# The first keys in two transfers, and two output tiles in one store

## The chip, the cores and the metric

The kernel runs on one core of one Trainium2 chip. The metric is the device time of one launch in microseconds (us). Several runs are made and their median counts.

## The reference, cut to what matters

Inputs: `q`, `k`, `v` of shape (8, 8, 576, 64) (batch, heads, sequence, head size), `phi` (512, 32), `w1` (8, 512, 1024), `w2` (8, 1024, 512), all float32. The output is (4608, 512) float32.

```
k_p, v_p = mean of k, v over groups of 8 neighbouring rows          # 576 -> 72 rows
attn     = softmax(q @ k_p^T / 8) @ v_p                             # pooled attention
x        = attn, heads side by side                                 # (4608, 512)
logits   = x @ phi                                                  # (4608, 32), 4 slots for each of 8 experts
d        = softmax of logits over the 4608 tokens
slots    = d^T @ x                                                  # 32 slot inputs
slot_out = relu(slots @ w1[e]) @ w2[e]   for the 4 slots of each expert e
out      = softmax of logits over the 32 slots  @  slot_out         # (4608, 512)
```

## The kernel before, in words

**Loads.** All of `q`, `k`, `v` and the weights are read once. Nearly all loads are issued by GpSimd (POOL), whose queue turns float32 into bfloat16 on the way; they stand in one queue (q0 in the profile) in the order of issue, and each is issued as soon as its buffer is free. `big` has four buffers for two batches (a "pair") of `q`, `k` or `v` each, 128 rows of 72 x 64 values; later the weights `w1` (`w_sb` in the profile) and `w2` follow, `w2` into buffers that the attention has left (`big`, `qTa`, `xsa`).

**The first keys.** One part of the first load goes another way. Of each of the 128 rows of pair 0 of `k`, the first `CUT` = 2048 values (8 KB of float32) are loaded by SyncE (SP; queue q1 in the profile) as float32 into `kf`, a piece of the tile `exa` that is not in use yet (L117 to L119). VectorE (DVE) and ScalarE (ACT) turn one half each into bfloat16 (L149, L150). The other 2560 values of each row come through POOL's queue (L120), and behind that load, in this order, stand the first `q`, `phi`, the first `v` and the second `k`. The engines meanwhile fill constants. TensorE (PE) begins when `phi` has been spread by DVE (L179): its first products are those of L184, between which the pooling of the first keys (L232) begins.

**Attention.** For each pair the keys and values are pooled and turned by PE, then scores (L309), exponentials (ACT, L311) and the product with the values (L331) run in a pipeline, written out in the order in which the engines are to work. PE's last use of a buffer releases POOL's next load.

**The end.** The last weights, of `w2`, come in two halves of 256 columns: first all pieces of the left half, then all of the right (L533). Into `so_ps` the second layer is summed. `begin(0, ...)` (L655) starts the output for the left half: it scales `so_ps` (`so_a`), makes the products of the first four tiles of 128 rows, scales them by `put` on ACT or DVE, and stores them with `store` (L635), which SP issues. `put(0)`, `put(1)` and `put(2)` of the left half are on ACT, one behind the other, `put(3)` is on DVE. Then `tiles` makes further left tiles, the right half's pieces are summed, `begin(1, ...)` starts the right half, and the remaining 26 tiles follow with all 512 columns and three large stores, of 8, 16 and 28 KB for each of 128 rows. A left or right tile is a store of 1 KB for each of 128 rows. All stores stand in q1.

**Order.** POOL's instructions, and from L546 those of all engines, stand in the order in which they are written; before that a planner orders the other engines, each of which then works in that order. A DMA counts up a semaphore when it has landed; SP's 16 DMAs use eight such semaphores in turn, so the ninth waits until the first has landed, and so on.

Of the kernel before, what the change touches and what calls it, by code (L numbers as in the profile page):

```python
# [18 lines left out]
def kernel(  # L19
# [10 lines left out]
    nc = tc.nc  # L30

    B, H, S, D = q.shape
# [51 lines left out]
    def pair_of(src, pair):  # L84
        return src[2 * pair:2 * pair + 2].rearrange("b h (i t) d -> (b h i) (t d)", t=NT)
# [30 lines left out]

    CUT = 4 * POOL * D  # L117
    kf = exf[:, 0:CUT]
    nc.sync.dma_start(out=kf, in_=pair_of(k, 0)[:, 0:CUT])  # L119
    nc.gpsimd.dma_start(out=big[:, 0, CUT:KQ], in_=pair_of(k, 0)[:, CUT:KQ])  # L120
    q_sb, k_sb, v_sb = {}, {}, {}
    k_sb[0] = big[:, 0].rearrange("p (t d) -> p t d", d=D)
# [41 lines left out]
    with tc.tile_pool(name="tmp", bufs=1) as tmp:  # L164
# [8 lines left out]
        for r in range(2):  # L173
            rows = slice(r * D, (r + 1) * D)
            nc.vector.tensor_copy(out=iphi[rows, :, r, 0:D],
                                  in_=ident[rows, rows].rearrange("p d -> p () d").to_broadcast([D, HQ, D]))
# [279 lines left out]
    def of_tile(t, n):  # L456
        g, r = TILES[n]
        rows, base = GROUPS[g]
        step, c0 = rows // 2, base // 2 + r // 2
        return t[:, r % 2, c0:c0 + 127 * step + 1:step]  # L460

    def tokens(n):

        return of_tile(cT, n)
# [64 lines left out]
    for half, cols in enumerate(halves):  # L529
        for e, j0, j1 in PIECES:  # L530
# [3 lines left out]
                                in_=moe_w2[e].rearrange("(p j) d -> p j d", j=FJ)[:, j0:j1, cols])  # L534
# [44 lines left out]
    def second_layer(e, j0=0, j1=FJ, half=None, by=1):  # L579

        cols = slice(0, DM) if half is None else halves[half]
        for fj in range(j0, j1):
            g = fj % NG
            rhs = w2_at[e, fj] if half is None else w2_half[e, fj, half]
            nc.tensor.matmul(out=so_ps[g * NS:(g + 1) * NS, cols].rearrange("p (c s) -> p s c", s=by), lhsT=hT[:, e, fj],  # L585
                             rhs=rhs.rearrange("p (c s) -> p s c", s=by),
                             start=(e == 0 and fj < NG), stop=(e == E - 1 and fj >= NG), skip_group_check=True)
# [29 lines left out]
    def scaled(engine, dst, src, by):  # L617
        if engine == 0:
            nc.scalar.activation(out=dst, in_=src, func=AF.Copy, scale=by)  # L619
        else:  # L620
            nc.vector.tensor_scalar(out=dst, in0=src, scalar1=by, scalar2=None, op0=ALU.mult)  # L621
# [13 lines left out]
    def store(g, r0, r1, cols):  # L635
        home, dst = places[g]
        nc.sync.dma_start(out=dst[:, r0:r1, cols], in_=home[:, r0:r1, cols])
# [13 lines left out]
    def put(n, cols, engine, ps):  # L651
        g, r = TILES[n]
        scaled(engine, places[g][0][:, r, cols], ps, rec(n))

    def begin(half, stores):  # L655

        cols = halves[half]
        scaled(0, so_a[:, cols], so_ps[:, cols], recC)
        f = []
        for n in range(CARRY):  # L660
            f.append(ps_f.tile([128, DM], FP, name="f_ps", tag="f")[:, 0:HC])
            nc.tensor.matmul(out=f[n], lhsT=of_tile(zT, n), rhs=w2_half[E - 1, J7, half],
                             start=True, stop=False)
        for n in range(CARRY):
            nc.tensor.matmul(out=f[n], lhsT=tokens(n), rhs=so_a[:, cols], start=False, stop=True)
            if n == (0 if half == 0 else CARRY - 1):
                second_layer(E - 1, J7, FJ, half)
        put(0, cols, 0, f[0])
        if half == 0:
            scaled(1, so[:, cols], so_ps[:, cols], recC)  # L670
            put(1, cols, 0, f[1])
            put(2, cols, 0, f[2])
            put(3, cols, 1, f[3])
        else:
            put(1, cols, 1, f[1])
            put(2, cols, 0, f[2])
            scaled(1, so[:, cols], so_ps[:, cols], recC)
            put(3, cols, 0, f[3])
        for r0, r1 in stores:
            store(0, r0, r1, cols)  # L680
# [22 lines left out]
    second_layer(*PIECES[1], 0)  # L703
    busy(192)
    second_layer(*PIECES[2], 0)
    begin(0, ((0, 1), (1, 2), (2, 4)))
    for n in (4, 6):
        tiles(n, n + 2, 0)
    for e, j0, j1 in PIECES[:2]:
# [42 lines left out]
```

## Time and profile before

| | us |
|---|---|
| median of 3 runs | 174.14 |
| lowest and highest | 174.07, 174.61 |
| the profiled execution, its own time | 174.13 |
| span of its instructions | 172.3 |
| PE busy | 131.0 |
| DVE busy | 100.6 |
| ACT busy | 88.1 |
| POOL busy | 27.5 |

The profile is of one execution. All times in it count from the first instruction of the program, and the execution's own time has 1.8 us more than the span, before and behind it. "DMA share" is the time that packets took as a share of 16 DMA engines; where two packets of one engine overlap it passes 1. GB/s counts the bytes that are written: for a load that turns float32 into bfloat16, half of what is read. A packet is here one row of a transfer.

### The profile page before, as it was taken

To read this page: it belongs to the slowest core of one execution; us is meant where nothing else is said; L and a number is where in the kernel's file an instruction comes from. 1 tells how busy PE (TensorE), PEld (TensorE's weight loads), DVE (VectorE), ACT (ScalarE), POOL (GpSimd) and SP (SyncE) were. 2 spreads that over 40 slices of the span, in tenths; PEclk is the share of its full clock that TensorE was granted. 3 is DMA by queue.
4 is the path that set the end of the run, shared out by engine and by line. 5 is a ranking of instruction groups with operands and counts; after the bars stand their busy time and mean duration, and the time that the engine had idled before them with its cause. 6 is when DMAs were issued, how large, how long until landed. Compare 5 with 4: busy or idle time off the path is not lost.

```text
span 172.3 us, 2868 instructions
## 1 busy us (share of the span) xinstructions
PE 131.0 (76%) x1106; PEld 70.1 (41%) x1106; DVE 100.6 (58%) x265; ACT 88.1 (51%) x168; POOL 27.5 (16%) x42
## 2 busy tenths in 40 slices
PE   0005778899999999999789999887899998799100
PEld 0002353565555655556345554462442235343000
DVE  6686263478779658887975868750650102599300
ACT  3201337977686937988503998555021004799100
POOL 7000111022101032207001471120501030000000
PEclk9999999999999999999999999999999999999955
DMA  5999999999999999999999999999999999999994
GB/s 184 252 218 225 210 216 220 215 216 214 214 216 220 209 224 208 220 218 216 215 213 215 217 213 221 215 219 219 215 215 215 206 196 195 322 369 436 479 426 213
DMA packets 10589, 41.13 MB, mean 239 GB/s; under 512 B 704, under 2 KB 6592, under 8 KB 6864
## 3 DMA queue, kind: packets, MB, share of 16 engines
q0 software_dynamic: 7248, 30.48, 87.1%
q1 hardware_dynamic: 3328, 10.49, 15.5%
q8 instruction: 8, 0.13, 0.3%
q14 instruction: 5, 0.04, 0.1%
HBM read 61.93 MB, written 9.44 MB: 414 GB/s over the span
## 4 chain that ended last, share of the span: by engine, by line
PE 33%; DMA 28%; DVE 15%; ACT 12%; issue 3%; POOL 1%; DVEq 0%; POOLq 0%; ACTq 0%
DMA xsa<-in_moe_w_dram 21%; PE pool_ps L232 10%; DMA phi_f<-in_moe_phi_dram 7%; ACT exa L311 7%; DVE xsa L342 6%; PE u_ps L331 5%; PE sc L309 5%; PE q_ps L264 4%; DVE w_sb L621 4%; PE G_ps L366 3%; PE turn_ps L248 2%; ACT vmeans L238 2%; DVE rsum L240 2%; ACT vp L296 2%; DVE rec L336 2%
## 5 line engine op out<-in xcount | busy, mean ns | idle before, releaser
L311 ACT ACTIVATE exa<-sc 72x576 bf16<-72x576 f32 x64 | 39.3, 653 | 4.6 <-PE sc L309 3.8
L342 DVE TENSOR_TENSOR xsa<-u_ps,rec 128x384 bf16<-128x384 f32 x69 | 37.8, 554 | 1.7
L331 PE MATMUL u_ps<-vp,exa 128*128 128x97 bf16 (+5 forms) x320 | 31.3, 229 | 3.6 <-DVE xsa L342 3.0
L331 PEld LDWEIGHTS <-exa 128*128 128x128 bf16 (+1 forms) x320 | 18.9, 100 | 15.7 <-DVE xsa L342 6.5
L309 PE MATMUL sc<-qTa,kp 64*72 64x288 bf16 x128 | 20.5, 303 | 1.7 <-ACT exa L311 1.3
L232 PE MATMUL pool_ps<-big,pmat 128*128 128x512 bf16 x64 | 18.2, 411 | 0.7 <-ACT qTa L268 0.6
L336 DVE RECIPROCAL rec<-u_ps 128x4 f32<-128x4 f32 x72 | 11.9, 175 | 10.8 <-PE u_ps L331 10.5
L184 PE MATMUL phi_ps<-spread,sel 128*128 128x256 bf16 x4 | 1.3, 396 | 15.0 <-DVE spread L179 15.0
L268 ACT COPY qTa<-q_ps 128x768 bf16<-128x768 bf16 x8 | 6.3, 794 | 12.3 <-PE q_ps L264 12.3
L621 DVE TENSOR_SCALAR w_sb<-f_ps,recR 128x512 f32<-128x512 f32 (+1 forms) x19 | 11.3, 660 | 1.5 <-DMA xsa<-in_moe_w_dram 0.7
L264 PE MATMUL q_ps<-ident,big 128*128 128x128 bf16 x144 | 11.6, 219 | 0.8 <-DVE qTa L270 0.3
L309 PEld LDWEIGHTS <-kp 64*72 64x72 bf16 x128 | 7.7, 106 | 8.9 <-issue 3.5
L240 DVE TENSOR_REDUCE rsum<-rest_ps 128x64 f32<-128x512 f32 x8 | 5.5, 692 | 10.0 <-PE rest_ps L236 9.9
L642 PE MATMUL f_ps<-so,cT 128*128 128x512 bf16 (+1 forms) x38 | 10.1, 361 | 1.6 <-DVE so L621 0.9
L619 ACT ACTIVATE w_sb<-f_ps,recR 128x512 f32<-128x512 f32 (+1 forms) x19 | 10.3, 620 | 1.3 <-PE f_ps L642 1.1
L270 DVE COPY qTa<-q_ps 128x768 bf16<-128x768 bf16 x16 | 8.7, 551 | 2.3 <-PE q_ps L264 2.2
L264 PEld LDWEIGHTS <-big 128*128 128x128 bf16 x144 | 8.7, 97 | 3.0 <-issue 1.4
L533 POOL DMA_DIRECT2D xsa<-in_moe_w_dram x8 | 5.9, 744 | 23.2 <-DMA qTa<-in_moe_w_dram 8.9
L366 PE MATMUL G_ps<-xsa,ee 128*128 128x512 bf16 x36 | 8.4, 379 | 1.2 <-ACT ee L361 1.2
L232 PEld LDWEIGHTS <-pmat 128*128 128x128 bf16 x64 | 6.0, 103 | 6.8 <-issue 2.3
L619 ACT ACTIVATE so_a<-so_ps,recC 128x256 bf16<-128x256 f32 x2 | 0.9, 474 | 13.8 <-PE so_ps L585 13.8
L238 ACT CAST vmeans<-pool_ps 128x1024 bf16<-128x1024 f32 x4 | 4.0, 1012 | 6.8 <-PE pool_ps L232 6.8
(109 smaller groups left out, 166.8 us busy)
## 6 DMA issues: line engine op xcount, KB each, us to landing
w_sb<-in_moe_w_dram POOLq DMA_DIRECT2D x2, 3072.0 KB, 37.6
big<-in_q_dram POOLq DMA_DIRECT2D x4, 1152.0 KB, 12.7
big<-in_v_dram POOLq DMA_DIRECT2D x4, 1152.0 KB, 16.5
big<-in_moe_w_dram POOLq DMA_DIRECT2D x1, 4096.0 KB, 34.2
out_dram<-w_sb SPq DMA_DIRECT2D x1, 3584.0 KB, 10.2
big<-in_k_dram POOLq DMA_DIRECT2D x3, 1152.0 KB, 21.3
w_sb<-in_moe_w_dram POOLq DMA_DIRECT2D x2, 1024.0 KB, 19.2
qTa<-in_moe_w_dram POOLq DMA_DIRECT2D x1, 2048.0 KB, 30.9
```

Of the source, the lines that this page charges most:

```text
L232: nc.tensor.matmul(out=ps, lhsT=pmat, rhs=src[:, t:full * POOL:POOL, :], start=(t == 0), stop=(t == POOL - 1))
L240: nc.vector.reduce_sum(out=rsum, in_=rest.rearrange("p t d -> p d t"), axis=AX.X)
L264: nc.tensor.transpose(out=ps[:, t].rearrange("p n i -> p (n i)"), in_=q_sb[pair][:, tt:tt + 2, :].rearrange("p t d -> p (t d)"), identity= ...
L309: nc.tensor.matmul(out=ps[:, r, 0:S // 2], lhsT=kp[pair][rows, n], rhs=qT[pair][rows, n].rearrange("p t i -> p (t i)"), start=True, stop=True)
L311: nc.scalar.activation(out=dst.rearrange("p r (i t) -> p r i t", t=NU), in_=ps[:, :, 0:S // 2].rearrange("p r (t i) -> p r i t", i=NI), fu ...
L331: nc.tensor.matmul(out=bank[rows, hh * UW:(hh + times) * UW].rearrange("p (a c) -> p a c", a=times), lhsT=ex[b][:, hh].rearrange("p r t -> ...
L336: nc.vector.reciprocal(out=rec, in_=ps[:, :, XW])
L342: nc.vector.tensor_tensor(out=dst, in0=ps[:, :, 0:XW], in1=rec.rearrange("p h -> p h ()").to_broadcast([128, HQ, XW]), op=ALU.mult)
L366: nc.tensor.matmul(out=ps, lhsT=ee[:, t].rearrange("p g s -> p (g s)"), rhs=x[:, t, :, 0:D], start=(t == 0), stop=(t == 8))
L619: nc.scalar.activation(out=dst, in_=src, func=AF.Copy, scale=by)
L621: nc.vector.tensor_scalar(out=dst, in0=src, scalar1=by, scalar2=None, op0=ALU.mult)
L642: nc.tensor.matmul(out=bank[:, 0:times * (cols.stop - cols.start)].rearrange("p (a c) -> p a c", a=times), lhsT=tokens(n), rhs=rhs.rearran ...
```

## The change

The load of the first keys by SP is cut in two: first 256 values (1 KB) of each of the 128 rows, then the other 1792 (7 KB) of each. The casts of L149 and L150 wait for both. And the left half of the first two output tiles, until now two stores, is stored by one. SP has 16 DMAs as before, and the order of the instructions on the other engines is the same.

```diff
     CUT = 4 * POOL * D
     kf = exf[:, 0:CUT]
-    nc.sync.dma_start(out=kf, in_=pair_of(k, 0)[:, 0:CUT])
+
+    AHEAD = 4 * D
+    for c0, c1 in ((0, AHEAD), (AHEAD, CUT)):
+        nc.sync.dma_start(out=kf[:, c0:c1], in_=pair_of(k, 0)[:, c0:c1])
     nc.gpsimd.dma_start(out=big[:, 0, CUT:KQ], in_=pair_of(k, 0)[:, CUT:KQ])
...
     second_layer(*PIECES[2], 0)
-    begin(0, ((0, 1), (1, 2), (2, 4)))
+    begin(0, ((0, 2), (2, 4)))
     for n in (4, 6):
         tiles(n, n + 2, 0)
```

## The prediction

> **What bounds the kernel now.** I read the page first, its slices, its queues and its chain, and then the DMA share by stretches of time.
>
> ```profile
> DMA  5999999999999999999999999999999999999994
> GB/s 184 252 218 225 210 216 220 215 216 214 214 216 220 209 224 208 220 218 216 215 213 215 217 213 221 215 219 219 215 215 215 206 196 195 322 369 436 479 426 213
> q0 software_dynamic: 7248, 30.48, 87.1%
> q1 hardware_dynamic: 3328, 10.49, 15.5%
> DMA xsa<-in_moe_w_dram 21%; PE pool_ps L232 10%; DMA phi_f<-in_moe_phi_dram 7%; ACT exa L311 7%; DVE xsa L342 6%; PE u_ps L331 5%; PE sc L309 5%; PE q_ps L264 4%; DVE w_sb L621 4%; PE G_ps L366 3%; PE turn_ps L248 2%; ACT vmeans L238 2%; DVE rsum L240 2%; ACT vp L296 2%; DVE rec L336 2%
> ```
>
> The reader is to see two things. In the DMA row only the first and the last slice are below 9. And q0 with 87.1% and q1 with 15.5% fill the 16 DMA engines for the whole span. The chain names many lines, but its largest piece is a load of weights, which lands when it does because everything ahead of it in the queue has been moved. By stretches:
>
> ```profile
> 1.00:1.50 0.50, 0.00 (x0) 0.00 (x0) 0.48 (x1) 0.50 (x1) 0.27 (x1) 1.00 0.00 0
> 1.50:2.00 0.50, 0.00 (x0) 0.00 (x0) 0.47 (x2) 0.50 (x1) 0.50 (x2) 1.00 1.28 213
> 1.50:2.50 1.00, 0.00 (x0) 0.00 (x0) 0.47 (x2) 0.72 (x2) 1.00 (x3) 1.00 0.86 164
> 2.50:3.50 1.00, 0.00 (x0) 0.00 (x0) 0.94 (x1) 0.00 (x0) 0.93 (x3) 1.00 0.81 295
> 3.50:4.50 1.00, 0.00 (x0) 0.00 (x0) 1.00 (x1) 0.00 (x0) 1.00 (x3) 1.00 1.01 426
> 5.50:8.50 3.00, 0.00 (x0) 0.00 (x0) 2.18 (x3) 1.04 (x1) 0.00 (x0) 1.00 1.09 225
> 24.00:128.00 104.00, 94.31 (x906) 54.82 (x906) 70.60 (x196) 68.69 (x132) 21.39 (x27) 1.00 1.03 216
> 150.00:151.00 1.00, 0.35 (x4) 0.36 (x4) 0.66 (x2) 0.78 (x3) 0.00 (x0) 1.00 0.98 342
> 154.00:170.00 16.00, 5.33 (x18) 2.10 (x17) 7.11 (x11) 6.09 (x11) 0.00 (x0) 0.78 1.06 445
> ```
>
> The last two columns are DMA share and GB/s. From 3.5 us to 170 us the share is 1 or above, with one stretch at 0.98. So the DMA engines are the bound, and the time is: when they reach full rate, plus bytes and packets over the rate. A microsecond that they lose or win at the start is carried to the end, and a microsecond of another engine counts only where it leaves them without work. That is the rule by which I cost both edits.
>
> **The start, as it is.** The queue view of the same stretches (packets, MB, share; 1.5 to 2.5, 2.5 to 3.5, 3.5 to 4.5, then both queues of 4.5 to 5.5), and who issues and who waits in the timeline:
>
> ```profile
> q1 hardware_dynamic: 20, 0.16, 86.1%
> q1 hardware_dynamic: 36, 0.29, 80.9%
> q1 hardware_dynamic: 52, 0.43, 101.0%
> q0 software_dynamic: 27, 0.14, 68.4%
> q1 hardware_dynamic: 36, 0.16, 39.5%
> ```
>
> ```profile
> 0.74 0.37 SPq L119 DMA_DIRECT2D exa<-in_k_dram  x1
> 1.23 0.67 POOL L120 DMA_DIRECT2D big<-in_k_dram  x1 [0.79 <-POOLq L736]
> 5.81 1.04 ACT L150 CAST big<-exa 128x1024 bf16<-128x1024 f32 x1 [3.58 <-DMA exa<-in_k_dram]
> 5.81 0.69 DVE L149 CAST big<-exa 128x1024 bf16<-128x1024 f32 x1 [0.94 <-DMA exa<-in_k_dram]
> 14.53 1.43 DVE L179 TENSOR_TENSOR spread<-phi_f,head 128x256 bf16<-128x256 f32 x4 [0.84 <-DMA phi_f<-in_moe_phi_dram]
> 15.01 0.71 PE L184 MATMUL phi_ps<-spread,sel 128*128 128x256 bf16 x2 [15.01 <-DVE spread L179]
> ```
>
> The first keys are issued at 0.74; nothing moves up to 1.5, and 8 KB packets begin between 1.5 and 2.0. I take 1.7, some 1.0 us after the issue. At full rate 52 packets begin in a microsecond, but only 20 and 36 did in the first two stretches. Counted from 1.7, the 1.8 us to 3.5 at 52 would be 94 packets and 56 came: 38 packets, or 0.7 us (an estimate from these rows) is lost while the engines run in. That is what the first edit can touch. POOL's queue moves nothing until SP's is nearly done, from 4.5.
>
> **The split.** SP issues two DMAs where it issued one, the second some 0.4 us behind, at about 1.1. Nothing else stands on SP's queue before the stores. Each of 16 engines gets eight packets of 1 KB and eight of 7 KB for eight of 8 KB. The price of a packet comes from two rates: 52 packets of 8 KB in 1 us are 16/52 = 0.308 us on one engine, and in the stretch of the 1 KB stores (148.5 to 154.5)
>
> ```profile
> DMA packets 2252, 2.15 MB, mean 359 GB/s; under 512 B 149, under 2 KB 2252, under 8 KB 2252
> ```
>
> 359 GB/s make 16 x 1024 / 359 = 45.6 ns. A line through both is 37.4 ns for a KB and 8 ns for a packet. Eight packets more on each engine cost 0.07 us, all of it on the path. This is my value for the packets, since it is from the same queue, though from stores. Dearer is the nearest row of small packets in loads, 144 to 146, where weights come in packets of 512 B:
>
> ```profile
> q0 software_dynamic: 788, 0.39, 145.1%
> ```
>
> 788 in 2 us are 41 ns each; a 1 KB packet at twice that (81 ns) would add 8 x (81 + 262 + 8 - 308), or 0.3 us. Below lies the case that the 1 KB packets run the engines in at little cost and the 7 KB packets then go at full rate: the whole 0.7 us comes back, less 0.07, so -0.6. Above lies the case that the second transfer is run in once more: +0.7 + 0.07. I take the lost 0.7 as it is, because it is a time at the start in which data come slowly, and short packets wait through it as long ones do: then the engines have moved less by 3 us, not more, and need the packets' 0.07 besides. The casts then begin at about 5.9 in place of 5.81. That costs nothing: they are hidden by the load of phi, for which DVE idles 0.84 us in front of L179.
>
> A rule of the Trainium skill speaks against this edit: "Perfetto Trace Analysis" (section DMA Optimizations) says that transfers under 2 KB carry much overhead each and are to be batched. It names no price there; in this trace the overhead is the 8 ns above, and by the rule alone the split would be a loss of unstated size.
>
> **The store.** The tail, with queue rows of 146 to 146.9 and then of 146.9 to 148.5:
>
> ```profile
> 145.22 1.27 ACT L619 ACTIVATE exa<-f_ps,recR 128x256 f32<-128x256 f32 x3 [0.36 <-PE f_ps L665]
> 145.72 1.32 SPq L637 DMA_DIRECT2D out_dram<-exa  x3
> 147.22 2.01 SPq L637 DMA_DIRECT2D out_dram<-w_sb  x3
> ```
>
> ```profile
> q0 software_dynamic: 356, 0.18, 144.5%
> q0 software_dynamic: 315, 0.15, 69.5%
> q1 hardware_dynamic: 326, 0.31, 56.2%
> ```
>
> Three `put`s on ACT take 1.27 us, so `put(1)` is done at about 145.22 + 2 x 0.42 = 146.1. The joint store waits for it: it is issued at about 146.1, 0.4 us later than the first store now, and as early as the second now. Queued behind it on SP is the store of tiles 2 and 3, which needs `put(2)` at 146.5 in any case, so it does not move. The bytes and the 1 KB packets stay the same, one issue of 0.4 us goes, and SP is not what the end waits for. Are DMA engines left idle by the 0.4 us? With 1.0 us from issue to packets, as at the start, the first store could have run at 146.7 and the joint one runs at 147.1. But until 146.9 no q1 packet ran at all: the loads still filled the engines, and 315 load packets came after that. Two tenths of a microsecond on the few engines that finish the loads first is the most that is lost, and those engines are not the last. I take 0, with +0.1 as the upper end. A small gain of 0.1 is possible if the last weights meet fewer stores.
>
> **The sum** against the profiled execution's own 174.13, which equals the median of 174.14: 0.07 for packets, 0 for the run-in, 0 for the casts, 0 for the store. That is 174.2. About 0.3%, or 0.5 us, is what a measurement of this kernel can tell from no change, as its runs reach from 174.07 to 174.61.
>
> **Rivals.** *The run-in shrinks (faster).* With 1 KB in front, all 128 rows are asked for within a short time, and whatever makes the first packets slow is waited for once for all eight of an engine rather than for the first and the second. For it speaks that the stretch 2.5 to 3.5 is still below the full 52 packets, although every engine should by then be past its first; against it, that the first bytes come no earlier. It gives at most 174.13 - 0.6 = 173.5. It decides the matter from about 80% of the lost 0.7 us on.
>
> *POOL's load gets between the two transfers (slower).* The first transfer is done on an engine at some time near 3; if POOL's load of L120 (issued at 1.23) is served before the 7 KB packets, the casts wait for it.
>
> ```profile
> big<-in_k_dram POOLq DMA_DIRECT2D x1, 640.0 KB, 7.6
> 136.00:138.20 2.20, 1.74 (x8) 0.52 (x9) 0.52 (x1) 0.00 (x0) 0.00 (x0) 1.00 0.99 199
> 141.00:144.00 3.00, 2.73 (x19) 1.39 (x18) 0.40 (x2) 0.00 (x0) 0.12 (x1) 1.00 1.45 195
> 144.00:146.00 2.00, 1.72 (x12) 0.99 (x12) 0.50 (x2) 1.26 (x3) 0.00 (x0) 1.00 1.45 196
> ```
>
> Its 0.655 MB at the 225 GB/s of 5.5 to 8.5 take 2.9 us. DVE works in order: the casts and all constants behind them move by 2.9, less the 0.84 of idle time, and PE begins 2.1 us later. The attention has no wait on a load in which this could vanish; PE's idle time of 0.46, 0.27 and 0.28 in the three rows takes up 1.0, and the first stores come 1.1 us late, when the loads have drained: the DMA engines stand idle that long. It gives 174.13 + 0.07 + 1.1 = 175.3. The point from which it counts is a cast later than 5.81 + 0.84 = 6.65. Against it speaks what is shown above: q1's stores, issued from 145.72 on, got no packet before 146.9 while q0 had work, and q0 got none before 4.5 while q1 had work. An engine seems to stay with a queue that has work, and the second transfer is there in time (issued at 1.1, so ready at 2.1). The Trainium skill ("DMA: Bandwidth & Descriptors", Queues, rings and completion order) has each DMA engine take its queues in turn, a packet of some 9 to 17 descriptors from each; by that rule a turn could end between the two transfers, and this rival would come true. The trace shows no such alternation in these two places.
>
> *The second transfer is run in anew (slower).* Its descriptors come late, or short rows pay the slow start each: +0.7 + 0.07, so 174.9.
>
> **Chances.** Forecast within 0.3%: 0.45. The run-in shrinks by enough: 0.28. POOL's load between: 0.12. A second run-in: 0.15. So faster 0.28, same 0.45, slower 0.27. The forecast's own bounds (-0.2 to +0.4) are 173.9 to 174.6; to hold eight in ten the range goes to 173.5 for the first rival and to 174.9 for the third, and leaves the 175.3 out.
>
> **What would show it.** Right: the stretch 1.5 to 3.5 again moves less than full rate, q1 is done at about 5.4, the casts begin between 5.8 and 6.1, PE begins at 15.0, the joint store is issued at about 146.1, and the DMA share stays at 1 to the end. Wrong towards faster: q0's packets begin by 4.2, and every landing after it is as much earlier. Wrong towards slower: q0 packets before q1's last, casts after 6.65, PE's start behind 15.5, or a share below 1 between 147 and 149, which would put the loss on the store.

## The result, and the profile after

| | before | after |
|---|---|---|
| median, us (22 runs each) | 174.16 | 174.31 |
| lowest to highest, us | 174.05 to 174.61 | 174.21 to 174.88 |
| span of the profiled execution, us | 172.3 | 172.5 |

The ratio after to before is 1.0013, with an interval of 1.0007 to 1.0019, which is 0.12 to 0.33 us. The change is a little slower, by less than the 0.3% that the forecast called no change.

The code behind the first edit has moved down by three lines: L119 and L120 are now L122 and L123, the casts are L152 and L153, `spread` is L182, and `store` issues from L640. The page after has the same two rows that showed the bound, the DMA slices and the two queues:

```profile
DMA  5999999999999999999999999999999999999994
q0 software_dynamic: 7248, 30.48, 87.1%
q1 hardware_dynamic: 3456, 10.49, 15.6%
```

q1 has 128 packets more, eight on each of 16 engines, and the engines are full as before. The chain of waits in time order (start, length, what) shows how a delay travels. Before, and then after:

```profile
140.53 8.18 DMA xsa<-in_moe_w_dram
148.76 0.61 PE f_ps L662 x4
160.45 0.66 DVEq L747
```

```profile
140.77 8.18 DMA xsa<-in_moe_w_dram
149.00 0.61 PE f_ps L665 x4
160.62 0.66 DVEq L750
```

The last weights land 0.24 us later, PE begins on them 0.24 later, and the last piece of the chain is 0.17 later. These weights are loaded by the same queue, in the same order and with the same bytes as before, so what they lost was lost ahead of them. Counted packet by packet in the two traces, POOL's queue has begun the same number of bytes 0.14 to 0.19 us later at 1, 2, 5, 10, 20 and 30 MB: the loss is there from the start and is carried along. The timeline of the changed kernel's start shows where:

```profile
0.74 0.84 SPq L122 DMA_DIRECT2D exa<-in_k_dram  x2
5.88 1.04 ACT L153 CAST big<-exa 128x1024 bf16<-128x1024 f32 x1 [3.63 <-DMA exa<-in_k_dram]
5.95 0.69 DVE L152 CAST big<-exa 128x1024 bf16<-128x1024 f32 x1 [1.08 <-DMA exa<-in_k_dram]
14.61 1.43 DVE L182 TENSOR_TENSOR spread<-phi_f,head 128x256 bf16<-128x256 f32 x4 [0.75 <-DMA phi_f<-in_moe_phi_dram]
15.09 0.70 PE L187 MATMUL phi_ps<-spread,sel 128*128 128x256 bf16 x2 [15.09 <-DVE spread L182]
```

The casts begin 0.07 to 0.14 later than the 5.81 of before, and PE 0.08 later than 15.01. And the queue view of the first microseconds (packets, MB, share; 1.5 to 2.5, 2.5 to 3.5, 3.5 to 4.5, then both queues of 4.5 to 5.5) stands against the five rows that the prediction shows of before:

```profile
q1 hardware_dynamic: 155, 0.22, 91.9%
q1 hardware_dynamic: 30, 0.21, 74.5%
q1 hardware_dynamic: 56, 0.40, 100.2%
q1 hardware_dynamic: 44, 0.22, 53.8%
q0 software_dynamic: 19, 0.10, 50.5%
```

A packet is counted, with all its bytes, in the stretch in which it begins. The share, times 16 engines and the length of the stretch, divided by the packets, is what one packet took: before, 0.69 us for 8 KB in the first stretch, 0.36 in the second and 0.31 in the third.

In the changed kernel the first stretch has all 128 packets of 1 KB (0.13 MB) and the first 12 of 7 KB; the other 15 are under 512 bytes. The 1 KB packets are slow at first too, as the row of 1.5 to 2.0 shows; the prediction's row of before has a share of 1.28 and 213 GB/s there:

```profile
1.50:2.00 0.50, 0.00 (x0) 0.00 (x0) 0.47 (x2) 0.50 (x1) 0.50 (x2) 1.00 0.26 51
```

That is 25 of them; the other 103 begin from 2.0 to 2.5. Then come the 7 KB packets, and in the second stretch they take 0.40 us each, against 0.29 in the third. By 3.5 us 0.43 MB have begun, against 0.45 before. By 5.5 us POOL's queue has begun 0.10 MB where it had begun 0.14; at the 225 GB/s that it writes from 5.5 to 8.5, the missing 0.04 MB are 0.18 us (an estimate, from rows that are rounded to 0.01 MB). That is about the whole loss.

The joint store of the tail and ACT's three `put`s ahead of it, with q0 and q1 of 146.9 to 148.5 behind it:

```profile
145.40 1.27 ACT L622 ACTIVATE exa<-f_ps,recR 128x256 f32<-128x256 f32 x3 [0.36 <-PE f_ps L668]
146.33 0.91 SPq L640 DMA_DIRECT2D out_dram<-exa  x2
```

```profile
q0 software_dynamic: 366, 0.17, 81.4%
q1 hardware_dynamic: 229, 0.23, 42.4%
```

The `put`s start at 145.40 in place of 145.22, the store leaves at 146.33, and q1 moves 229 packets in that stretch, against the 326 of before. With the joint store alone it is 294, so the store's wait is one part of this; the other is that loads and `put`s come later. The stores by themselves are measured below.

### The profile page after: what moved, and what is told of

Same layout as the page of the kernel before. It is cut to its first block, busy times and chain, and to the rows that moved or that the text cites. A ratio compares the mean times of both kernels' runs of the same rounds, so it can differ in the third digit from the quotient of the medians.

```text
span 172.5 us, 2869 instructions
## 1 busy us (share of the span) xinstructions
PE 130.8 (76%) x1106; PEld 70.1 (41%) x1106; DVE 100.6 (58%) x265; ACT 88.1 (51%) x168; POOL 27.6 (16%) x42
## 4 chain that ended last, share of the span: by engine, by line
PE 33%; DMA 28%; DVE 15%; ACT 13%; issue 3%; POOL 1%; DVEq 0%; POOLq 0%; ACTq 0%
DMA xsa<-in_moe_w_dram 21%; PE pool_ps L235 10%; DMA phi_f<-in_moe_phi_dram 7%; ACT exa L314 7%; DVE xsa L345 6%; PE u_ps L334 5%; PE sc L312 5%; PE q_ps L267 4%; DVE w_sb L624 4%; PE G_ps L369 3%; PE turn_ps L251 2%; ACT vmeans L241 2%; ACT vp L299 2%; DVE rec L339 2%; ACT qTa L271 1%
```

## The experiments: which part costs

All edits are against the kernel before, unless the text says otherwise. The change has two parts, so each was done alone, and each was measured against the kernel before. In microseconds, an interval is the ratio's times 174.1.

**The split alone.** SP then has 17 DMAs in place of 16.

```diff
-    nc.sync.dma_start(out=kf, in_=pair_of(k, 0)[:, 0:CUT])
+    AHEAD = 4 * D
+    for c0, c1 in ((0, AHEAD), (AHEAD, CUT)):
+        nc.sync.dma_start(out=kf[:, c0:c1], in_=pair_of(k, 0)[:, c0:c1])
```

> The split of the first keys alone, the stores as before. If the measured +0.15 us comes from the split, this is +0.10 to +0.20 against the kernel before, phi lands 0.1 later and the casts begin at about 5.9. If it comes from the joint store, this is +0.07 at most, which is the price of 8 packets more on each engine at 8 ns.

Measured: 174.69 against 174.17, ratio 1.0031 (1.0021 to 1.0041). That is +0.52 us, more than the whole change, and more than the +0.10 to +0.20 that was expected.

**The joint store alone.** SP then has 15 DMAs.

```diff
-    begin(0, ((0, 1), (1, 2), (2, 4)))
+    begin(0, ((0, 2), (2, 4)))
```

> The joint store alone, the first keys in one transfer. If the split is the cause: 0.00 +- 0.05. If the store is: +0.10 to +0.15, and the DMA share between 147 and 149 is lower than before.

Measured: 174.21 against 174.17, ratio 1.0001 (0.9992 to 1.0010). The joint store costs and brings nothing that can be measured (-0.14 to +0.17 us). So the parts do not add up: +0.52 and 0.0 alone, and +0.15 together. The profile of the split alone gives the reason. At the end of the program SP waits until every DMA has landed. First its instructions of that kind on the last line, with the times of the first and the last; before, then the split alone:

```profile
L747 SPq EVENT_SEMAPHORE  x4: 17/22/28, 163.0 to 172.3; - x4
...
L747 SPq DRAIN  x3: 7/7/7, 171.5 to 171.8; - x3
```

```profile
L749 SPq EVENT_SEMAPHORE  x10: 17/28/28, 171.6 to 172.9; - x10
...
L749 SPq DRAIN  x3: 7/7/7, 172.1 to 172.4; - x3
```

Then the waits of SP from 162 us on (total, times, longest), before and the split alone:

```profile
SPq L747 <- DMA out_dram<-w_sb: 9.4, 2, 8.4
```

```profile
SPq L749 <- DMA out_dram<-w_sb: 9.8, 1, 9.8
```

In each row the last two instructions stand behind the first drain; the 2 and the 8 ahead of it are the ends of waits. The 16 DMAs use eight semaphores in turn, so before, the last store is on the eighth. SP waits for the eight one after another; the long wait that began at 163.0 ends 8.4 us later, at 171.4, and the drain follows at 171.5. With 17 DMAs the last store is on the first semaphore. SP waits for that one until 171.6, and goes through the other seven, all long done, before its drain at 172.1: 0.5 us from the landing to the drain in place of 0.1. The rest of the +0.52 lies ahead of the landing, which is at 171.6 in place of 171.4. The joint store brings the number back to 16 and so takes the waits away: in the changed kernel the long wait ends at 171.60 and the drain comes at 171.66.

**Seventeen DMAs without the split.** That reading was tested by adding a store and leaving the load whole.

```diff
-    begin(0, ((0, 1), (1, 2), (2, 4)))
+    begin(0, ((0, 1), (1, 2), (2, 3), (3, 4)))
```

> The first keys in one transfer as before, but the left half of tiles 2 and 3 in two stores, so 17 DMAs by SP. The theory is now: the split costs 0.1 to 0.15 us; and at the end SP waits for its eight DMA semaphores one after the other, 0.06 us each, and with 17 DMAs the last store stands on the first of them, so that seven waits more come after its landing. Then this is +0.42 (7 x 0.06) without any split, and ten SP semaphore instructions stand at the end from 171.5 on. If the 0.37 that split_only is slower than the change comes from the split and a gain by the joint store instead, this is +0.05 at most.

Measured: 174.53 against 174.14, ratio 1.0023 (1.0014 to 1.0032), +0.39 us. In its chain the piece of the last weights and the last piece start within 0.02 us of where they start before, but the drain comes at 171.9:

```profile
140.55 8.17 DMA xsa<-in_moe_w_dram
...
160.43 0.66 DVEq L747
```

```profile
L747 SPq EVENT_SEMAPHORE  x10: 17/28/28, 171.4 to 172.7; - x10
...
L747 SPq DRAIN  x3: 7/7/7, 171.9 to 172.2; - x3
```

So the 0.39 us lie wholly behind the last landing: seven waits of 0.06 us each (0.39 divided by seven; in the trace the eight waits end from 171.43 to 171.86, 0.06 apart). It is shown that the second part of the change takes away what the first would cost at the end.

## The experiments: the slow start of the first packets

What is left of the change, 0.12 to 0.33 us, should by the prediction be 0.07 for packets, with the run-in as before. Three kernels vary the pieces; two of them keep the joint store, and so 16 DMAs.

**The long piece first** (the changed kernel, 7 KB and then 1 KB).

```diff
-    for c0, c1 in ((0, AHEAD), (AHEAD, CUT)):
+    for c0, c1 in ((AHEAD, CUT), (0, AHEAD)):
```

> The same two transfers as in the change, in the other order: 7 KB of each row first, then 1 KB; joint store. The same packets, so +0.07 if their number is the price. If the change's further loss is that 1 KB in front does not end the slow start, which the 7 KB packets then pay as well, this is +0.05 to +0.10 and below the change; if any second transfer costs 0.15, it is +0.15.

Measured: 174.19 against 174.14, ratio 1.0002 (0.9993 to 1.0011), +0.05 us. It has as many packets as the changed kernel, of the same sizes. If the order matters to nothing else, the price of 128 packets more lies between -0.12 and +0.19; the prediction's 0.07 is in it, and so is nothing at all.

**Two halves of 4 KB** (the changed kernel with `AHEAD` at 16 x D).

```diff
-    AHEAD = 4 * D
+    AHEAD = 16 * D
```

> The first keys in two transfers of 4 KB of each row, and the joint store, so 16 DMAs. By the waits at the end: halves was +0.44, less 0.42, so +0.02 to +0.10: the price of the packets (0.07), as the first long packets are slow once. If a second transfer costs by itself whatever its size: +0.15 like the change.

Measured: 174.36 against 174.14, ratio 1.0012 (1.0003 to 1.0021), +0.22 us. That is above the +0.02 to +0.10 of the first expectation, but its interval (0.05 to 0.37) takes in a part of that, and the +0.15 of the other.

**Two halves, stores as before** (17 DMAs).

```diff
-    nc.sync.dma_start(out=kf, in_=pair_of(k, 0)[:, 0:CUT])
+    AHEAD = 16 * D
+    for c0, c1 in ((0, AHEAD), (AHEAD, CUT)):
+        nc.sync.dma_start(out=kf[:, c0:c1], in_=pair_of(k, 0)[:, c0:c1])
```

> The first keys in two transfers of 4 KB of each row: as many packets as 1 KB and 7 KB. Price of packets: +0.07 us. If the run-in is a stretch of time, the same as the split (+0.10 to +0.20), with the slow packets in the first transfer and none in the second; if a transfer's first long packets are slow, packets of both transfers are and it is +0.3 or more.

Measured: 174.61 against 174.17, ratio 1.0025 (1.0015 to 1.0035), +0.44 us. Against the two halves with 16 DMAs this is 0.22 more, where the seven waits would add 0.39; the intervals (0.26 to 0.61, and 0.05 to 0.37) leave room for that. In its trace the waits are there in full (the last landing is seen at 171.5, the drain comes at 172.0); the last store lands 0.16 earlier than in the kernel with 16 DMAs, and why is not known. So the +0.3 or more of the expectation came, but by the waits; it was to come from slow packets in both transfers.

None of the three comes out faster than before. The queue rows of the long piece first (1.5 to 2.5, 2.5 to 3.5, 3.5 to 4.5) show the run-in again:

```profile
q1 hardware_dynamic: 17, 0.12, 86.6%
q1 hardware_dynamic: 48, 0.34, 86.5%
q1 hardware_dynamic: 60, 0.38, 92.9%
```

Here the long packets begin at once and are slow in the first stretch (0.12 MB); in the changed kernel they begin behind the short ones and are slow in the second (0.21 MB). The slowness follows the long packets, and a short piece ahead of them does not take it away. Whether the order matters beyond that isn't settled: +0.15 with 1 KB first and +0.05 with 7 KB first have intervals that overlap. One profile of each kernel points that way. From 4.5 to 5.5 POOL's queue begins 19 and 17 packets with 1 KB first (the changed kernel and the split alone), 23, 23 and 28 with the other two-piece loads, and 25 to 28 with the load in one piece. If so, the +0.15 is the slow start that became a little longer, and not the price of packets.

**No load by SP at all.** POOL loads the whole first pair of keys, and the two casts go.

```diff
-    nc.sync.dma_start(out=kf, in_=pair_of(k, 0)[:, 0:CUT])
-    nc.gpsimd.dma_start(out=big[:, 0, CUT:KQ], in_=pair_of(k, 0)[:, CUT:KQ])
+    nc.gpsimd.dma_start(out=big[:, 0, 0:KQ], in_=pair_of(k, 0)[:, 0:KQ])
...
-    nc.vector.tensor_copy(out=big[:, 0, 0:CUT // 2], in_=kf[:, 0:CUT // 2])
-    nc.scalar.copy(out=big[:, 0, CUT // 2:CUT], in_=kf[:, CUT // 2:CUT])
```

> No transfer by SP at the start: the whole first load of k goes through POOL's queue, and the two casts are gone. It shows when POOL's queue can begin and whether its first packets are slow too. If POOL's queue was ready early (by 3 us) and only kept waiting by SP's packets: it begins before 3 and the time is about +0.3 to +1.3, since the start is later by that much. If it is ready only at about 4.5: +2.8.

Measured: 175.50 against 174.16, ratio 1.0078 (1.0063 to 1.0093), +1.34 us, at the top of the +0.3 to +1.3 that was expected if POOL's queue is ready by 3 us. Its stretches of time, with DMA share and GB/s in the last two columns, tell two things:

```profile
2.00:2.50 0.50, 0.00 (x0) 0.00 (x0) 0.00 (x0) 0.22 (x2) 0.50 (x2) 1.00 0.00 0
2.50:3.00 0.50, 0.00 (x0) 0.00 (x0) 0.44 (x1) 0.00 (x0) 0.42 (x3) 1.00 2.49 258
3.00:4.00 1.00, 0.00 (x0) 0.00 (x0) 1.00 (x1) 0.00 (x0) 1.00 (x3) 1.00 0.48 65
4.00:5.00 1.00, 0.00 (x0) 0.00 (x0) 0.81 (x2) 0.00 (x0) 0.61 (x2) 1.00 0.85 175
5.00:6.00 1.00, 0.00 (x0) 0.00 (x0) 0.69 (x1) 0.00 (x0) 0.00 (x0) 1.00 0.97 203
```

First, POOL's load, issued at 1.24, is ready to run between 2.5 and 3.0, some 1.3 to 1.8 us after its issue, where SP's is ready about 1.0 us after. Second, its first packets are slow in turn. From 2.5 to 3.0 the 258 GB/s are 14 packets of 9 KB that begin there, and a share of 2.49 makes 1.4 us for each, where from 5 to 6 one takes 0.7 us. The 65 GB/s of 3 to 4 are that low because these 14 still hold the engines. From 3.5 on SP's long packets run at full rate in the changed kernel. So the run-in isn't a fixed stretch of time at the start of the program, as the prediction took it. It comes with the first long packets of the program, in whichever queue they are. It does not come again with the second queue's first: the prediction's row of before has 27 packets of POOL's from 4.5 to 5.5 at 68.4%, which is 0.41 us each, and from 5.5 to 8.5 they take 0.40. What makes the first long packets slow isn't known.

## The experiments: POOL's load between the two

The stretch above also says that the second rival was close: POOL's queue can run from 2.5 on, and in the changed kernel the second transfer, issued at about 1.15, is ready at about 2.2. Three kernels make the later pieces of SP late. The first two have 17 DMAs, so about 0.4 us of what they lose are the waits at the end.

**The second transfer late.** It is held back until ACT has made its first activation, which writes into its destination; to that end the zeros are made earlier. (The planner then also sets DVE's cast later in DVE's order, behind more of the constants.)

```diff
-    nc.sync.dma_start(out=kf, in_=pair_of(k, 0)[:, 0:CUT])
+    AHEAD = 4 * D
+    nc.sync.dma_start(out=kf[:, 0:AHEAD], in_=pair_of(k, 0)[:, 0:AHEAD])
+    nc.vector.memset(hT, 0.0)
+    zeros = hT.rearrange("p e j s -> p (e j s)")[:, 0:512]
+    nc.scalar.activation(out=kf[:, AHEAD:AHEAD + 1], in_=zeros[:, 0:1], func=AF.Exp)
+    nc.sync.dma_start(out=kf[:, AHEAD:CUT], in_=pair_of(k, 0)[:, AHEAD:CUT])
...
-    nc.scalar.activation(out=dummy, in_=zeros[:, 0:1], func=AF.Exp)
```

> The split with the 7 KB transfer issued only when ACT's first activation is done, at about 2.3 in place of 1.1 (its packets can begin at 3.3). If POOL's queue is ready before 3.3, its load gets between the two: the casts begin at about 8.7 or later and PE's start and the time move by up to 1.1 us, if nothing hides it. If POOL's queue is not ready by then, the engines stand idle from 2.4 to 3.3, the casts begin at about 6.8, and the time is +0.9.

Measured: 179.21 against 174.16, ratio 1.0299 (1.0279 to 1.0319), +5.05 us. That is far more than the 1.1 that was expected at most. POOL's next load in the kernel before, then this kernel's timeline, its queues from 9 to 12 us, and two stretches of time:

```profile
20.20 0.53 POOL L100 DMA_DIRECT2D big<-in_q_dram  x1 [15.60 <-PE rest_ps L236]
```

```profile
2.26 0.33 SPq L124 DMA_DIRECT2D exa<-in_k_dram  x1
...
14.31 1.04 ACT L151 CAST big<-exa 128x1024 bf16<-128x1024 f32 x1 [12.08 <-DMA exa<-in_k_dram]
...
20.65 0.71 PE L185 MATMUL phi_ps<-spread,sel 128*128 128x256 bf16 x2 [20.65 <-DVE spread L180]
...
25.52 0.54 POOL L100 DMA_DIRECT2D big<-in_q_dram  x1 [20.90 <-PE rest_ps L237]
```

```profile
q0 software_dynamic: 53, 0.49, 77.2%
q1 hardware_dynamic: 51, 0.37, 30.3%
```

```profile
20.00:24.00 4.00, 3.35 (x10) 1.41 (x10) 2.13 (x7) 0.52 (x2) 0.00 (x0) 1.00 1.02 214
24.00:28.00 4.00, 2.80 (x25) 1.61 (x24) 1.96 (x4) 1.28 (x3) 0.54 (x1) 1.00 0.59 97
```

An issue 1.1 us later makes the casts 8.5 us late. POOL's first load has begun by the time SP's second transfer is ready, and it runs through: from 3.5 to 5.5 POOL's queue begins 74 packets and SP's none. From about 6 on the two queues are served row by row, 53 against 51 from 9 to 12. The trace shows the turns themselves: from 9 to 11 the starts repeat every 0.96 us, with 16 rows of each queue, so each engine takes one row of SP's (0.29 us) and one of POOL's (0.70) in turn. PE begins 5.6 us late. It then releases the buffer for POOL's next load at 25.52 in place of 20.20, the loads in the queue have run out by then, and the engines stand at 0.59 from 24 to 28: 1.6 us lost in this one stretch. The remaining 3 us are not worked out piece by piece.

**Three pieces** (the changed kernel, of 1, 1 and 6 KB).

```diff
-    for c0, c1 in ((0, AHEAD), (AHEAD, CUT)):
+    for c0, c1 in ((0, AHEAD), (AHEAD, 2 * AHEAD), (2 * AHEAD, CUT)):
```

> The first keys in three transfers: 1, 1 and 6 KB of each row, joint store (17 DMAs). SP issues the third at about 1.9, so it is ready at about 2.9, when the first two are done and POOL's queue is ready (2.5 to 3.0 in all_by_pool). If POOL's load gets in front and the two queues then take turns: the casts begin after 12 and the time is +4 to +6 as in second_late. If the third transfer is still in time on all engines: +0.2 for packets, +0.42 for the waits at the end, so +0.6.

Measured: 177.24 against 174.14, ratio 1.0160 (1.0118 to 1.0203), +3.10 us. There are four runs, and they scatter from 175.89 to 177.92, so only the direction is sure, and the size is rough. It is below the +4 to +6 that was expected for this case. Its timeline, and POOL's queue from 2.5 to 3.0:

```profile
0.74 1.33 SPq L122 DMA_DIRECT2D exa<-in_k_dram  x3
...
10.36 1.04 ACT L153 CAST big<-exa 128x1024 bf16<-128x1024 f32 x1 [8.12 <-DMA exa<-in_k_dram]
...
18.24 0.71 PE L187 MATMUL phi_ps<-spread,sel 128*128 128x256 bf16 x2 [18.24 <-DVE spread L182]
...
149.12 1.03 SPq L640 DMA_DIRECT2D out_dram<-exa  x2
```

```profile
q0 software_dynamic: 10, 0.05, 135.3%
```

Three issues take 1.33 us, so the third leaves at about 1.65, half a microsecond behind the second, and that is already too late. The attention begins 3.2 us late and the first left store, a joint one as in the changed kernel, is 2.8 us behind the 146.33 there. The margin of the changed kernel is thus at most half a microsecond of issue time.

POOL's first ten packets begin before 3.0 here. In the changed kernel its load is issued at the same 1.24, and it begins nothing before 4.5, while SP's 7 KB rows, which came first, run through. So a load that comes first can be served to its end, here SP's and with the second transfer late POOL's first, eight rows on each engine both times; the turns are seen for what comes later. What decides between the two isn't known. In this kernel no single stretch shows the engines idle as clearly as above; where its 3.1 us are lost piece by piece is not worked out.

**Eight pieces of 1 KB, stores as before.**

```diff
-    nc.sync.dma_start(out=kf, in_=pair_of(k, 0)[:, 0:CUT])
+    AHEAD = 4 * D
+    for c0, c1 in [(c, c + AHEAD) for c in range(0, CUT, AHEAD)]:
+        nc.sync.dma_start(out=kf[:, c0:c1], in_=pair_of(k, 0)[:, c0:c1])
```

> The first keys in eight transfers of 1 KB of each row, so 56 packets more on each engine. If the price is that of packets (8 ns each) and the run-in is a time at the start that is lost in any case: +0.45 us. If each transfer is run in anew, by 0.1 us each: +0.45 + 0.7 = +1.15. If the slow start belongs to long packets alone (8 or 7 KB), so that 1 KB packets go at full rate from the first: 0.7 less, so -0.25. In the queue view the stretch 2.5 to 3.5 then starts about 350 packets of 1 KB; if the chip is slow at that time whatever is sent, about 200.

Measured: 193.17 against 174.17, ratio 1.1075 (1.1048 to 1.1102), +19.0 us. This was meant to price small packets, and priced the rival instead. The queues from 3.5 to 4.5, the last cast, and a stretch of time:

```profile
q0 software_dynamic: 18, 0.09, 60.2%
q1 hardware_dynamic: 14, 0.01, 7.0%
```

```profile
27.00 1.04 ACT L152 CAST big<-exa 128x1024 bf16<-128x1024 f32 x1 [24.77 <-DMA exa<-in_k_dram]
```

```profile
28.00:32.00 4.00, 0.00 (x0) 0.00 (x0) 3.03 (x7) 0.05 (x1) 0.00 (x0) 1.00 0.00 0
```

On 16 engines 18 and 14 packets in a microsecond are about one of each queue per engine. From 9 to 11 us the starts repeat every 0.74 us, with 16 rows of each queue: one row of POOL's (0.70 us) and one of SP's (0.06). Each short row pays for a long row of POOL's, and there are many short rows. The keys are complete at 27 us; the engines then have nothing to load (share 0.00 from 28 to 36) until the attention has begun and released a buffer.

In the three kernels the loss is about as long as POOL's next load is late: it leaves at 23.42 with three pieces, at 25.52 with the second transfer late and at 39.99 with eight pieces, in place of 20.20. That is 3.2, 5.3 and 19.8 us, against +3.1, +5.05 and +19.0.

## Why the prediction was right, and where it wasn't

**The bound and its rule: right.** What is lost at the start is found again in the landing of the last weights (+0.24) and at the end (+0.17); and what delays only the attention costs when it leaves the DMA engines without work. (By shorter stretches the share is at times a little below 1, as 0.97 from 156 to 158 before; that changes nothing.)

**The sum: right in size.** It was +0.07 and came out at +0.15, with an interval of 0.12 to 0.33. The packets' term of 0.07 is within what the long piece first allows (-0.12 to +0.19), but no run tells it from nothing. The joint store's term of 0 is within its run alone (-0.14 to +0.17), and its issue at 146.33 is about the forecast 146.1 and the 0.18 that the `put`s themselves start late. The casts at 5.88 and 5.95 and PE at 15.09 are where they were put. Whether what is over the 0.07 belongs to the packets, to a longer run-in or to the measurement is open.

**The run-in: about the right number, for a reason that holds only in part.** The prediction kept the lost 0.7 us because short packets would wait through a slow time at the start. They did so for a part of it: 25 began before 2.0 us, at a share of 0.26. But the other 103 came in the next half microsecond, and the rest of the loss is paid when the 7 KB packets begin, at 0.40 us each, and in the run without SP's load by POOL's. That the two parts together come to about what was lost before is luck. The first rival (faster) fell because the long packets are slow behind the short ones too: none of the orders tried was faster than before. The third rival (a second run-in, +0.77) was too dear, since the slow start comes once, with the first long packets.

**POOL's load between the transfers: a premise that holds here and not in general.** The prediction held that an engine stays with a queue that has work. In the changed kernel it does: POOL's queue begins nothing before 4.5. The tail, its other place, was weak support: with 1.0 us from issue to packets the first store is ready only at 146.7, and from 146.9 on the prediction's own rows have both queues, 315 and 326. But with three pieces, eight pieces and the second transfer late it does not: there each engine comes to take one row of each queue in turn, 26 against 24 (three pieces, 4.5 to 5.5), 18 against 14 and 53 against 51. The Trainium skill ("DMA: Bandwidth & Descriptors", Queues, rings and completion order) says that an engine "round-robins between the queue rows it has work for", some 9 to 17 descriptors at a time. These runs agree with the turns; their length there is one row of the profile, shorter than the page says, if a row is one descriptor. The eight rows of a load that runs through are near the page's lower figure; whether they are such a turn no run shows. What saved the forecast is the other half of the argument, that the second transfer is there in time, and the margin for that is half a microsecond at most. The rival's price of 1.1 us was too low: about 3.1, 5.05 and 19.0 where it came true. The price missed two things: that the waiting rows are served only in turn with POOL's, so the casts came 4.5 us late and more, not 2.9; and that a late attention releases POOL's next loads late, which the prediction counted only at the stores.

**What was not in it.** The semaphores at the end. The front of the document had the eight in turn, and the forecast noted neither that 16 is a good number nor that the split alone would break it. It did no harm, since the change keeps 16.

## What to carry to other kernels

Where the DMA engines are the bound, cutting a load brought nothing by itself; ask what stands behind it in the other queue and how long after, for half a microsecond decided here between almost nothing and some 3 us. Count a queue's DMAs against its semaphores: when the last one to land isn't the last one waited for, the other waits come behind the end. And when two small edits come together, run each alone, since one may be there to pay for the other.

## What the runs showed of the hardware that was not expected

- Seven waits on semaphores that had long been reached cost 0.39 us at the program's end, 0.06 us each.
- The first long packets of the program are slow whichever queue has them: 0.69 us for 8 KB of SP's in the stretch 1.5 to 2.5 before (0.31 at full rate), 0.40 for 7 KB behind the 1 KB packets in 2.5 to 3.5 after (0.29), 1.4 for 9 KB of POOL's when SP loads nothing (0.7). POOL's first packets behind SP's long ones are not slow (0.41, then 0.40). The cause is open.
- Two queues with work can be served one row each in turn on each engine, whatever the rows' sizes: 18 packets of POOL's and 14 of SP's in a microsecond on 16 engines moved 0.09 and 0.01 MB. A queue of short rows then gets almost nothing beside a queue of long ones. A load that came first can run through instead: in the changed kernel POOL's queue begins nothing before 4.5, though the same load begins before 3.0 with three pieces.
